# Searched orders for a gated recurrence and a causal convolution on one core: which engine gates the input, and in which order each engine works

## The chip, the cores and the metric

The kernel runs on one core of a Trainium2 chip. A core has TensorE (PE) for matmuls, VectorE (DVE), ScalarE (ACT) for activations, GpSimd (POOL), and SyncE (SP), which here issues the loads and stores. Each engine works through its own queue in order, and the engines wait for each other through semaphores. The metric is the device time of one execution in microseconds (us). The kernel before took 312.61 us, the median of 6 runs (311.6 to 314.11).

## The reference, cut to what matters

The input has 4 sequences of 6336 steps with 256 channels, 25344 rows in all. First comes a gated linear recurrence:

```python
log_a = c * sig_r * np.log(np.clip(a_base, 1e-06, 1.0 - 1e-06))[None, None, :]
a_t = np.exp(log_a)
norm = np.sqrt(np.maximum(1.0 - a_t * a_t, 1e-06))
x_gated = norm * sig_i * x
for t in range(S):
    h = a_t[:, t] * h + x_gated[:, t]
    y[:, t] = h
```

Its output goes through a causal convolution of five taps per channel, whose sigmoid gates a projection, and through an output projection:

```python
for k in range(K):
    gate_pre += conv_w[k][None, None, :] * xp[:, k:k + S, :]
gate = 1.0 / (1.0 + np.exp(-gate_pre))
val = x @ w_val
return (gate * val @ w_out).astype(np.float32)
```

## The kernel before, in words

Rows are cut into 51 tiles of 512 (three of them have 256), and tiles into 28 chunks of one or two tiles. Chunk 0 is tile 0, chunk 1 is tile 1, chunk 2 is tiles 2 and 3, and so on. Steps on channels-by-time data work by chunk and by half (`h` = 0 or 1, 128 channels each), numbered k = 2 x chunk + half. Square roots work by batches of two chunks, 14 in all.

A tile goes through these steps, named as in the code:

- `load` (L264, two DMAs for the two gates) and `loadx` (L271), issued by SP; `tanh` on ScalarE (L348) makes both gates.
- `u2` gates the input: (1 + tanh) times x. The string `U2` has one letter for each tile. With P, GpSimd does it in two instructions, L363 and L364. With D, VectorE does it in one fused instruction (L359) for each half of a tile.
- `srT` on TensorE (L373) transposes a gate, `exp` on ScalarE (L382) makes the decay a, `e` on GpSimd (L390) squares it, and `sq` on ScalarE (L394) takes the root for a batch. The root needs another activation table than `tanh` and `exp`, so there is a table load of 1.28 us before and after each `sq`.
- `nT` (L404) transposes the norm back, `xg` on VectorE (L411) multiplies it with the gated input, `xT` (L420) transposes the product, and `scan` on VectorE (L438) runs the recurrence.
- `conv` (L464, TensorE), `tg` (L472, ScalarE), `val` (L480, TensorE), `gv` (L490, VectorE), `out` (L502, TensorE); then the eviction `osb`, on VectorE (L513) or ScalarE (L515) by the letters of the string `OSB`, one for each half tile; and `store` (L520, SP).

The order of each engine's queue is written out as a string of letters in `ORDER`, one string for each engine; a letter stands for the next job of its kind on that engine. `make_plan` checks that the strings do not wait for each other. Its costs (`COST`) set only the order in which the instructions of different engines are emitted. Four PSUM banks serve `srT`, `nT`, `xT` and `out`, in the order of `BANK_ORDER`: a transpose into a bank waits until the earlier content has been read, that is for an `exp`, `xg`, `scan` or `osb`.

Buffers add waits. `tanh` of tile g writes the input gate's place of tile g - 5, so it waits for `u2` of that tile. `loadx` of tile g waits for `u2` of tile g - 4, and `load` for `tanh` of tile g - 4. `store` waits for its evictions, and what stands behind it on SP waits with it. The weights of the two projections are loaded by six DMAs that GpSimd issues (L527, L530), directly behind `e` 1 in its queue.

Of the kernel before, what the change touches and what calls it, by code (L numbers as in the profile page):

```python
# [29 lines left out]
BANKS = 4  # L30
PB = dict(srT=2, nT=2, xT=2, ops=2)

OSB = "DDDDDDDDDDDDDDDDDDDDDDDDDDDDDDDDDDDDDDDDDDDDDDDDDDDDDADDDDDDDDDDDDDDDDDDDDAAAAADDDDDAAAAAAAAAAADADA"

U2 = "DDDDPDPDDPPPPPPPPPPPDPPPPPPPPPPPPPPPPPPPPPPPPPPPPPP"

COST = dict(load=(0.05, 2.72), loadx=(0.02, 1.37), tanh=(0.11, 1.7), u2P=(0.2, 3.25), u2D=(0.2, 1.7), srT=(0.05,
            0.47), exp=(0.26, 0.86), e=(0.06, 1.83), sq=(0.2, 1.71), nT=(0.05, 0.53), xg=(0.02,
            0.58), xT=(0.04, 0.46), scan=(0.13, 2.14), conv=(0.15, 1.08), tg=(0.1, 0.83), val=(0.02,
            0.88), gv=(0.07, 1.07), out=(0.02, 0.43), osbD=(0.6, 0), osbA=(0.5, 0), store=(0.03,  # L40
# [3 lines left out]
LETTERS = dict(  # L44
    DMA=dict(l="load", x="loadx", s="store"), ACT=dict(t="tanh", e="exp", q="sq", g="tg", o="osb"),
    PE=dict(r="srT", n="nT", x="xT", c="conv", v="val", o="out"), POOL=dict(e="e", u="u2"),
    DVE=dict(u="u2", x="xg", s="scan", v="gv", o="osb"))
ORDER = dict(
    DMA=("lllxlllxlxlxxlxlxxlllxxlxlxsxxlsxlxllssxxlslxsxsllxxlsxssllslsxxxlsllssxslxlslsxxsllxslxslsxxsxslllx"
         "slxsxssllxlxxsxsslslxllsxsxsxllsxslxssxsxxsssssssssss"),  # L50
    ACT=("teeteetqtteteetetgqteegtteettgqgetegetetgqgteegttgetegtgeqgteetgetgqgetettgeegtgqeegttgtegetgtegqegt"
         "tgeetgtegqegttegetgoetgqegttegetgqgetegtgetgetgqeogetgootgoeoteegeqgeogeoqogogoogogooooggoo"),
    PE=("rrrrrrnxnrxrcxvxrcvrnnxnrxrnoocxxvcornrnvnocorxronvcxvooxcxronnvrocnovxncrvxroocxrocvooxvocrononcxrn"
        "voroxconvxocvornonnrcvonxrxvorcoxocovroxvxcrvnooncooxvrocxrvocnnoorcoovxcoorvnxvonocrxvrocoxvnrocono"
        "vxoxcrvonnocxrrxvoocnnrxcovroxovconvonnxrxcrnovcxroocvoxooovcrnnonxocxrvcrvoncovoxocovronxvrnncxnovo"
        "cxroovxrrcorovxoocovnonrcxrovonxcxnnvxocovocxxovcoxovooxcovcovoo"),
    POOL="eeeeeeeeueueeeuuueeeeuuuueeeueuuueeeeuueeeeuuueeuueeuueueueeueueueueeuueueeuuueeueeuuueueeeeuueeeuu",
    DVE=("uxsuxsussuvxuxusxsvxooussovxxvxoosxovsvoosoxxsovoxvxssoovsoovosovooxxusxvoosoxvsooxoxvxvxossovoosoov"
         "svsxooxvoosvosoxovoxoovsoovxsoxvosvoosovxoxovossxxovossoxxvsovosovxooxvxssxovsoovoosoovxxoxsovsvxoov"
         "oosovxsxxvsxvsvsoovoosoxxvsvxsxxvssvssvsvsovvo"))  # L60
BANK_ORDER = ("2123321110130102331302130221230122302301230123012121132131023123012102312123210310103201301301320131"
              "2023103130123102130231201213202310203123132010303132031321023031231202302001302313021231120312310321"
              "20131232130321320112030212312010312032010301231210212310312231")

WEIGHTS_AFTER = ("e", 1)
TABLE, SEM, DMA_LAT = 1.3, 0.15, 2.2
# [2 lines left out]
BF16 = mybir.dt.bfloat16  # L69
ACT = mybir.ActivationFunctionType  # L70
ALU = mybir.AluOpType
# [60 lines left out]
def make_jobs(sh):  # L132
# [9 lines left out]
    def job(op, eng, f, deps, cost=None, bank=0):  # L142
        fix, per = COST[cost or op]
        jobs[op].append((eng, fix + per * f, [d for d in deps if d[1] >= 0], bank))

    for g, (_, n) in enumerate(sh.tiles):
        f = n / WIN
        c = sh.chunk_of[g]
        job("load", "DMA", f, [("tanh", g - NIN)])
        job("loadx", "DMA", f, [("u2", g - NX)])  # L150
        job("tanh", "ACT", f, [("load", g), ("u2", g - NTI)]
            + ([("srT", 2 * sh.chunk_of[g - NTR] + 1)] if g >= NTR else []))
        job("u2", "DVE" if U2[g] == "D" else "POOL", f, [("tanh", g), ("loadx", g)] + ([("xT", 2 * sh.chunk_of[g - NU] + 1)] if g >= NU else []), "u2" + U2[g])
        job("nT", "PE", f, [("sq", unit_of[c]), ("xg", g - PB["nT"])], None, 1)
        job("xg", "DVE", f, [("nT", g), ("u2", g)])
        job("conv", "PE", f, [("scan", 2 * c + 1), ("tg", g - 1)])
        job("tg", "ACT", f, [("conv", g), ("gv", g - 2)])
        job("val", "PE", f, [("scan", 2 * c + 1), ("gv", g - 1), ("conv", g)])
        job("gv", "DVE", f, [("tg", g), ("val", g)] + ([("out", qlast[g - 2])] if g >= 2 else []))
        job("store", "DMA", f, [("osb", q) for q, (w, _) in enumerate(sh.pieces) if w == g])  # L160
    for c, (_, n, g0, g1) in enumerate(sh.chunks):
# [3 lines left out]
        for h in range(2):  # L165
            k = 2 * c + h
            job("srT", "PE", f, [("tanh", g1 - 1), ("exp", k - PB["srT"])], None, 1)
            aold = ("scan", 2 * sh.aold[c] + h if sh.aold[c] >= 0 else -1)
            job("exp", "ACT", f, [("srT", k), aold])
            job("e", "POOL", f, [("exp", k), ("sq", eu), ("nT", sh.chunks[ed][3] - 1 if ed >= 0 else -1)])  # L170
            job("xT", "PE", f, [("xg", g1 - 1), ("scan", k - PB["xT"])], None, 1)
            job("scan", "DVE", f, [("xT", k), ("val", ylast - 1), ("conv", ylast)])
    for q, (g, i) in enumerate(sh.pieces):
        job("out", "PE", 1, [("gv", g), ("osb", q - PB["ops"])], None, 1)
        job("osb", "DVE" if OSB[q] == "D" else "ACT", 1, [("out", q), ("store", g - NOSB)], "osb" + OSB[q])
    for u, n in enumerate(UNITS):
        size = sum(sh.chunks[c][1] for c in range(ends[u] - n, ends[u])) / CHUNK
        fix, per = COST["sq"]
        jobs["sq"].append(("ACT", fix * len(sh.runs[u]) + per * size, [("e", 2 * ends[u] - 1)], 0))
# [3 lines left out]
def make_plan(sh):  # L183
# [5 lines left out]
    for eng, letters in ORDER.items():  # L189
        todo = {op: [i for i, job in enumerate(jobs[op]) if job[0] == eng] for op in LETTERS[eng].values()}  # L190
        seq[eng] = [(op, todo[op].pop(0)) for op in (LETTERS[eng][x] for x in letters)]
        assert not any(todo.values())
    free_bank = iter(BANK_ORDER)
    for op, i in seq["PE"]:
# [5 lines left out]
    done, order, mode = {}, [], "E"  # L200
    free = dict(dict.fromkeys(seq, 0.0), DMA=START, ACT=ACT_START)
    at, left = dict.fromkeys(seq, 0), sum(len(ops) for ops in seq.values())
    while left:
        was = left
        for eng, ops in seq.items():
            while at[eng] < len(ops):
# [9 lines left out]
                free[eng] = t + dur  # L216
                done[op, i] = t + dur + (DMA_LAT if eng == "DMA" else 0.0)
                order.append((t, op, i, eng, dur))
# [351 lines left out]
```

## Time and profile before

| what | us |
|---|---|
| median of the runs | 312.61 |
| the profiled execution | 312.68 |
| its span, from the first to the last instruction | 310.8 |
| ScalarE busy | 289.1 |
| VectorE busy | 272.1 |
| TensorE matmul busy | 244.5 |
| GpSimd busy | 243.6 |
| DMA: share of 16 engines' time of the main queue | 88.2% |

Times in the profile count from the span's start. A group's row gives the line, the engine, the operation, what it writes and reads, the count, the busy time and mean nanoseconds, and then the idle time of the engine just before these instructions, with what ended it. In a timeline, each row has start, length, engine, line, operation, and in brackets the idle time before. In the 40 slices one digit stands for the busy tenths of 7.8 us.

### The profile page before, as it was taken

Reading aid. Unit: us, or ns where it says so; the run is one execution under the profiler, and the core shown is the slowest. Engines: PE = TensorE matmul, PEld = TensorE weight load, DVE = VectorE, ACT = ScalarE, POOL = GpSimd, SP = SyncE. Lnnn points to the kernel's source line nnn. Section 1 sums busy time; section 2 is a strip of 40 time slices with the busy share of each in tenths; the row PEclk is TensorE's granted clock in tenths of the full one; section 3 lists DMA queues with packets and bytes.
Section 4 is the critical chain, followed back from the end, with each engine's and each line's share of the span. In section 5 each row is a group of like instructions: output and inputs, shape, how many; then the busy total and the mean of one; then the engine's idle time right before and its main releaser. Section 6 shows DMA issues by size and latency. Waiting matters only on the chain.

```text
span 310.8 us, 6573 instructions
## 1 busy us (share of the span) xinstructions
PE 244.5 (79%) x2559; PEld 160.7 (52%) x2591; DVE 272.1 (88%) x279; ACT 289.1 (93%) x225; POOL 243.6 (78%) x154
## 2 busy tenths in 40 slices
PE   1127565789788858987899889888897998999994
PEld 1115243466555545654566555555564766656563
DVE  3008957989999999999999989999999899999973
ACT  6799699999999996999999999999999999999762
POOL 0907719999998999549999999899999989987300
PEclk9999897999999997999999999999999999999999
DMA  6999999999899999699999999997989999673145
GB/s 224 399 370 390 368 310 402 394 372 414 280 365 351 345 365 410 223 366 421 372 331 358 356 419 418 412 392 271 390 310 331 363 418 413 248 263 136 70 182 226
DMA packets 30797, 104.51 MB, mean 336 GB/s; under 512 B 4391, under 2 KB 4654, under 8 KB 30766
## 3 DMA queue, kind: packets, MB, share of 16 engines
q1 hardware_dynamic: 29376, 103.82, 88.2%
q0 software_dynamic: 1376, 0.26, 1.0%
q8 instruction: 20, 0.33, 0.4%
q14 instruction: 11, 0.09, 0.1%
q10 hardware_dynamic: 14, 0.01, 0.0%
HBM read 78.39 MB, written 25.95 MB: 336 GB/s over the span
## 4 chain that ended last, share of the span: by engine, by line
ACT 24%; DVE 21%; DMA 16%; issue 13%; PE 13%; POOL 10%; SPq 2%; DVEq 0%; ACTq 0%; POOLq 0%
DVE yring L438 9%; DMA ri<-in_i_gate_dram 8%; ACT tring L348 7%; ACT aring L382 5%; DMA out_dram<-osb 5%; POOL uring L364 5%; ACT ering L394 4%; DVE osb L513 4%; DVE gv L490 4%; PE gp L464 4%; PE bank L502 3%; ACT tg L472 3%; POOL ering L390 3%; POOL t L363 2%; DVE uring L411 2%
## 5 line engine op out<-in xcount | busy, mean ns | idle before, releaser
L390 POOL TENSOR_TENSOR ering<-aring 128x1024 f32<-128x1024 f32 (+2 forms) x56 | 95.2, 1714 | 40.9 <-ACT aring L382 40.1
L438 DVE TENSOR_TENSOR_SCAN yring<-aring,yring,bank 128x1024 bf16<-128x1024 f32 (+5 forms) x54 | 110.0, 2050 | 3.0 <-PE bank L420 2.9
L364 POOL TENSOR_TENSOR uring<-t,xt 128x1024 bf16<-128x1024 f32 (+1 forms) x43 | 100.1, 2328 | 3.6
L348 ACT ACTIVATE tring<-ri 128x2048 bf16<-128x2048 f32 (+1 forms) x51 | 94.2, 1868 | 3.7 <-issue 2.6
L464 PE MATMUL gp<-yring,diag 64*64 64x512 bf16 (+14 forms) x1196 | 67.5, 353 | 2.4 <-ACT tg L472 1.8
L382 ACT ACTIVATE aring<-bank,khf 128x1024 f32<-128x1024 bf16 (+2 forms) x56 | 61.1, 1111 | 3.7 <-PE bank L373 3.1
L502 PE MATMUL bank<-wo,gv 128*128 128x256 bf16 x396 | 58.6, 276 | 6.9 <-DVE yring L438 2.1
L490 DVE SCALAR_TENSOR_TENSOR gv<-tg,val 128x1024 bf16<-128x1024 bf16 (+1 forms) x54 | 60.4, 1122 | 2.7 <-PE val L480 2.0
L472 ACT ACTIVATE tg<-gp 128x1024 bf16<-128x1024 f32 (+1 forms) x51 | 51.3, 1007 | 5.2 <-PE gp L464 4.4
L373 PE MATMUL bank<-ident_b,tring 128*128 128x128 bf16 x396 | 34.5, 231 | 27.4 <-ACT tring L348 19.2
L513 DVE TENSOR_SCALAR osb<-bank 128x512 f32<-128x512 f32 x80 | 52.8, 679 | 3.2 <-PE bank L502 2.1
L480 PE MATMUL val<-yring,wv 128*128 128x512 bf16 (+1 forms) x172 | 47.7, 376 | 4.1 <-DVE gv L490 2.0
L502 PEld LDWEIGHTS <-gv 128*128 128x128 bf16 x396 | 36.7, 99 | 24.3 <-issue 11.5
L394 ACT ACTIVATE ering<-ering,b 128x4096 bf16<-128x4096 f32 (+4 forms) x16 | 46.8, 2934 | 0.2
L411 DVE TENSOR_TENSOR uring<-bank,uring 128x1024 bf16<-128x1024 bf16 (+1 forms) x51 | 33.2, 665 | 15.4 <-PE bank L404 15.2
L363 POOL TENSOR_SCALAR t<-tring 128x1024 f32<-128x1024 bf16 (+1 forms) x43 | 45.0, 1046 | 1.7
L373 PEld LDWEIGHTS <-tring 128*128 128x128 bf16 x396 | 28.0, 104 | 35.3 <-ACT tring L348 20.8
L464 PEld LDWEIGHTS <-diag 64*64 64x64 bf16 x1196 | 30.9, 109 | 27.7 <-issue 13.0
L404 PE MATMUL bank<-ident_f,ering 128*128 128x128 f32 x198 | 34.9, 304 | 12.5 <-ACT ering L394 5.6
L404 PEld LDWEIGHTS bank<-ident_f,ering 128*128 128x128 f32 x198 | 27.8, 207 | 20.3 <-ACT ering L394 7.7
L420 PE MATMUL bank<-ident_f,uring 128*128 128x128 f32 x198 | 33.6, 288 | 5.6 <-DVE uring L411 2.4
L420 PEld LDWEIGHTS bank<-ident_f,uring 128*128 128x128 f32 x198 | 22.8, 145 | 16.2 <-DVE uring L411 4.6
(32 smaller groups left out, 106.2 us busy)
## 6 DMA issues: line engine op xcount, KB each, us to landing
ri<-in_r_gate_dram SPq DMA_DIRECT2D x48, 512.0 KB, 7.7
ri<-in_i_gate_dram SPq DMA_DIRECT2D x48, 512.0 KB, 8.2
xt<-in_x_dram SPq DMA_DIRECT2D x48, 512.0 KB, 8.4
out_dram<-osb SPq DMA_DIRECT2D x48, 512.0 KB, 6.1
ri<-in_r_gate_dram SPq DMA_DIRECT2D x3, 256.0 KB, 6.2
ri<-in_i_gate_dram SPq DMA_DIRECT2D x3, 256.0 KB, 7.6
xt<-in_x_dram SPq DMA_DIRECT2D x3, 256.0 KB, 5.1
out_dram<-osb SPq DMA_DIRECT2D x3, 256.0 KB, 2.1
```

What stands on the lines that cost most here:

```text
L348: nc.scalar.activation(out=tring[:, r:i + 1:i - r, 0:nj, :], in_=ri[:, :, 0:nj, :], func=ACT.Tanh, scale=0.5)
L364: nc.gpsimd.tensor_tensor(out=u.rearrange("p w d e -> p w e d"), in0=t1.rearrange("p (w e) d -> p w e d", e=2), in1=xt.rearrange("p (w e) ...
L373: nc.tensor.transpose(out=srT[:, col:col + P], in_=tring[:, g % NTR, j, h * P:(h + 1) * P], identity=ident_b[:])
L382: nc.scalar.activation(out=aring[:, h, a0:a0 + nt].rearrange("c (w p j) -> c w p j", p=P, j=nj), in_=live.pop(("srT", k))[:, 0:nt].rearran ...
L390: nc.gpsimd.tensor_tensor(out=ering[:, H * e0 + h * nt:H * e0 + (h + 1) * nt], in0=a, in1=a, op=ALU.mult)
L404: nc.tensor.transpose(out=nT[:, w * D + h * P:w * D + (h + 1) * P], in_=ering[:, n0 + w:n0 + nw * P:nw], identity=ident_f[:])
L438: nc.vector.tensor_tensor_scan(out=yring[:, h, y0 + c0:y0 + c1], data0=aring[:, h, a0 + c0:a0 + c1], data1=xT[:, c0:c1], initial=0.0 if fr ...
L464: nc.tensor.matmul(out=gp[64 * h:64 * h + 64, m, c0:c1], lhsT=diag[rows, h, kk, rows], rhs=yring[rows, h, src:src + c1 - c0], start=(sh == 0),
L472: nc.scalar.activation(out=tg[:, :, 0:nt], in_=live.pop(("gp", g))[:, :, 0:nt], func=ACT.Tanh, scale=0.5)
L490: nc.vector.scalar_tensor_tensor(out=gv[:, 0:nj, hs, :].rearrange("c j h p -> c j (h p)"), in0=tg[:, hs, 0:nt].rearrange("c h (p j) -> c j ...
L502: nc.tensor.matmul(out=ops[:, e * D:(e + 1) * D], lhsT=gv[:, 2 * i + e, hk, :], rhs=wo[:, hk, :], start=(hk == 0), stop=(hk == H - 1))
L513: nc.vector.tensor_scalar(out=dst, in0=ops[:], scalar1=0.5, scalar2=None, op0=ALU.mult)
```

## The change

Three letters of `U2` go from D to P: tiles 5, 8 and 20. VectorE keeps the gated input of tiles 0, 1, 2, 3 and 7. Nine letters of `OSB` change; VectorE has 79 evictions instead of 80. The planner's cost of a gated input on VectorE goes from (0.2, 1.7) to (0.3, 3.3). With these, all five orders and the order of the banks are other strings. The work itself, the tiles, the buffers and the batches of roots stay.

```diff
-OSB = "DDDDDDDDDDDDDDDDDDDDDDDDDDDDDDDDDDDDDDDDDDDDDDDDDDDDDADDDDDDDDDDDDDDDDDDDDAAAAADDDDDAAAAAAAAAAADADA"
+OSB = "DDDDDDDDDDDDDDDDDDDDDDDDDDDDDDDDDDDDDDDDDDDDDADDDDDDDDDDDDDDDDDDDDDDDDDDAAAAADDAAAAAADDAAAAAADADA"
-U2 = "DDDDPDPDDPPPPPPPPPPPDPPPPPPPPPPPPPPPPPPPPPPPPPPPPPP"
+U2 = "DDDDPPPDPPPPPPPPPPPPPPPPPPPPPPPPPPPPPPPPPPPPPPPPPPP"
-... u2D=(0.2, 1.7) ...
+... u2D=(0.3, 3.3) ...
 ORDER = dict(
-    DMA=("lllxlllxlxlxxlxlxxlllxxlxlxsxxlsxlxllssxxlslxsxsllxxlsxssllslsxxxlsllssxslxlslsxxsllxslxslsxxsxslllx"
+    DMA=("lllxlxllxllxxlxxllxllxxlxxxllssllsxsxxsllxslxllsxlssxlxxslxslxlsxslsxxllsxxlxssxslslllxsslsxxsllxsls"
...
-    ACT=("teeteetqtteteetetgqteegtteettgqgetegetetgqgteegttgetegtgeqgteetgetgqgetettgeegtgqeegttgtegetgtegqegt"
+    ACT=("teteeetqtteteeetgtqgettetegetgqteetgteegttegqgettgetegetqgteegettgqgetetgtegetgqeegtgttgeegtgqegettg"
...
-    PE=("rrrrrrnxnrxrcxvxrcvrnnxnrxrnoocxxvcornrnvnocorxronvcxvooxcxronnvrocnovxncrvxroocxrocvooxvocrononcxrn"
+    PE=("rrrrnrnrxxrcrxxrvcvnnnxrxnrcroxocvrxoonovnrnxcnrocxrvocorovxocoxvrnnncxrvornxcrovoooxcovnrnxvorcrxvo"
...
-    POOL="eeeeeeeeueueeeuuueeeeuuuueeeueuuueeeeuueeeeuuueeuueeuueueueeueueueueeuueueeuuueeueeuuueueeeeuueeeuu",
+    POOL=("eeeeeeeeuuueeeeuuuueeeeuueueueeuueueeeuuuueeeeuueueueeuuueueueeeuueueeuuueeueueuuueeeuuueeeueuueeuu"
+          "ee"),
-    DVE=("uxsuxsussuvxuxusxsvxooussovxxvxoosxovsvoosoxxsovoxvxssoovsoovosovooxxusxvoosoxvsooxoxvxvxossovoosoov"
+    DVE=("uuxxssussvuxxxssxvuosovsoxooxxvsoxsvooovsoosxxvxsoxvsoovoosovxxsvosovsooxxovosxoovxsovosoovxxvoosoxs"
...
-BANK_ORDER = ("2123321110130102331302130221230122302301230123012121132131023123012102312123210310103201301301320131"
+BANK_ORDER = ("2023201312203123013103020312313010301320102020323213023213101323232312023132320131302312012302131001"
...
```

At the start, ScalarE's order "teeteetq" becomes "teteeetq": `exp` 1 stands behind `tanh` 1. VectorE's "uxsuxsuss" becomes "uuxxssuss". At the end, GpSimd's last two gated inputs stand ahead of the last two `e` instead of behind them, and ScalarE's queue has 13 jobs behind the last root instead of 17.

More of the change, by code (lines that the diff above doesn't have):

```diff
@@ L31 @@
 PB = dict(srT=2, nT=2, xT=2, ops=2)
-OSB = "DDDDDDDDDDDDDDDDDDDDDDDDDDDDDDDDDDDDDDDDDDDDDDDDDDDDDADDDDDDDDDDDDDDDDDDDDAAAAADDDDDAAAAAAAAAAADADA"
-U2 = "DDDDPDPDDPPPPPPPPPPPDPPPPPPPPPPPPPPPPPPPPPPPPPPPPPP"
-COST = dict(load=(0.05, 2.72), loadx=(0.02, 1.37), tanh=(0.11, 1.7), u2P=(0.2, 3.25), u2D=(0.2, 1.7), srT=(0.05,
+OSB = "DDDDDDDDDDDDDDDDDDDDDDDDDDDDDDDDDDDDDDDDDDDDDADDDDDDDDDDDDDDDDDDDDDDDDDDDAAAAADDDAAAAAADDAAAAAADADA"
+U2 = "DDDDPPPDPPPPPPPPPPPPPPPPPPPPPPPPPPPPPPPPPPPPPPPPPPP"
+COST = dict(load=(0.05, 2.72), loadx=(0.02, 1.37), tanh=(0.11, 1.7), u2P=(0.2, 3.25), u2D=(0.3, 3.3), srT=(0.05,
             0.47), exp=(0.26, 0.86), e=(0.06, 1.83), sq=(0.2, 1.71), nT=(0.05, 0.53), xg=(0.02,
@@ L48 @@
 ORDER = dict(
-    DMA=("lllxlllxlxlxxlxlxxlllxxlxlxsxxlsxlxllssxxlslxsxsllxxlsxssllslsxxxlsllssxslxlslsxxsllxslxslsxxsxslllx"
-         "slxsxssllxlxxsxsslslxllsxsxsxllsxslxssxsxxsssssssssss"),
-    ACT=("teeteetqtteteetetgqteegtteettgqgetegetetgqgteegttgetegtgeqgteetgetgqgetettgeegtgqeegttgtegetgtegqegt"
-         "tgeetgtegqegttegetgoetgqegttegetgqgetegtgetgetgqeogetgootgoeoteegeqgeogeoqogogoogogooooggoo"),
-    PE=("rrrrrrnxnrxrcxvxrcvrnnxnrxrnoocxxvcornrnvnocorxronvcxvooxcxronnvrocnovxncrvxroocxrocvooxvocrononcxrn"
-        "voroxconvxocvornonnrcvonxrxvorcoxocovroxvxcrvnooncooxvrocxrvocnnoorcoovxcoorvnxvonocrxvrocoxvnrocono"
-        "vxoxcrvonnocxrrxvoocnnrxcovroxovconvonnxrxcrnovcxroocvoxooovcrnnonxocxrvcrvoncovoxocovronxvrnncxnovo"
-        "cxroovxrrcorovxoocovnonrcxrovonxcxnnvxocovocxxovcoxovooxcovcovoo"),
@@ L57 @@
-    POOL="eeeeeeeeueueeeuuueeeeuuuueeeueuuueeeeuueeeeuuueeuueeuueueueeueueueueeuueueeuuueeueeuuueueeeeuueeeuu",
-    DVE=("uxsuxsussuvxuxusxsvxooussovxxvxoosxovsvoosoxxsovoxvxssoovsoovosovooxxusxvoosoxvsooxoxvxvxossovoosoov"
-         "svsxooxvoosvosoxovoxoovsoovxsoxvosvoosovxoxovossxxovossoxxvsovosovxooxvxssxovsoovoosoovxxoxsovsvxoov"
-         "oosovxsxxvsxvsvsoovoosoxxvsvxsxxvssvssvsvsovvo"))
-BANK_ORDER = ("2123321110130102331302130221230122302301230123012121132131023123012102312123210310103201301301320131"
-              "2023103130123102130231201213202310203123132010303132031321023031231202302001302313021231120312310321"
-              "20131232130321320112030212312010312032010301231210212310312231")
+    DMA=("lllxlxllxllxxlxxllxllxxlxxxllssllsxsxxsllxslxllsxlssxlxxslxslxlsxslsxxllsxxlxssxslslllxsslsxxsllxsls"
+         "xxlxssllxslxssxslxlxlslsxssxxllssxxslsxssxsxsssssssss"),
@@ new lines @@
+    ACT=("teteeetqtteteeetgtqgettetegetgqteetgteegttegqgettgetegetqgteegettgqgetetgtegetgqeegtgttgeegtgqegettg"
+         "tegetogetgqetgtegetgqegtetgtegetgeqgetgtgetgetgqooegetogeoteogetegeqoogoogoeogqgoogogoooggoo"),
+    PE=("rrrrnrnrxxrcrxxrvcvnnnxrxnrcroxocvrxoonovnrnxcnrocxrvocorovxocoxvrnnncxrvornxcrovoooxcovnrnxvorcrxvo"
+        "cxnnoovoocxrvnocorxnovrxocrvoocnnvooxcronxrvnoxcxvocroxrcvncoovronoovoxrcnvxnoocvnrxcorvocoxrvoncoox"
+        "ocxorvnnnvxrocrnvocxvxorcoxoovnronocxvrrocoxvconrnovooxrcxonvcnovxcorxcrovncoonvoorxvoconnxvrxoncnvr"
+        "xocroovrorcxrxvocoovnnonoxcovxorcoovxcxvnonocxovcxoxvoxocovcovoo"),
@@ new lines @@
+    POOL=("eeeeeeeeuuueeeeuuuueeeeuueueueeuueueeeuuuueeeeuueueueeuuueueueeeuueueeuuueeueeueuuueeeuuueeeueuueeuu"
+          "ee"),
+    DVE=("uuxxssussvuxxxssxvuosovsoxooxxvsoxsvooovsoosxxvxsoxvsoovoosovxxsvosovsooxxovosxoovxsovosoovxxvoosoxs"
+         "xovsosovsvxoovoxoovosxvxoosxvsoovsovxoosoovxxsxvosxvossoovosxovxoosvoosvoxxovososxvoxovssovoxooxvoos"
+         "vxxsvxsxvsovosovsxxxvsvsovosxvsxsvssvsvovo"))
+BANK_ORDER = ("2023201312203123013103020312313010301320102020323213023213101323232312023132320131302312012302131001"
+              "0131203212320031202312302320323011321031231012310232123102012310321132031320132032103021302232310120"
+              "13202312012023100213320321031330231023010230210320030320130132")
```

## The prediction

> **What bounds the kernel now.** I read the busy shares first, then the 40 slices, then the waits of ScalarE and GpSimd, then the timelines around ScalarE's two longest holes. The page:
>
> ```profile
> span 310.8 us, 6573 instructions
> PE 244.5 (79%) x2559; PEld 160.7 (52%) x2591; DVE 272.1 (88%) x279; ACT 289.1 (93%) x225; POOL 243.6 (78%) x154
> DVE  3008957989999999999999989999999899999973
> ACT  6799699999999996999999999999999999999762
> POOL 0907719999998999549999999899999989987300
> L382 ACT ACTIVATE aring<-bank,khf 128x1024 f32<-128x1024 bf16 (+2 forms) x56 | 61.1, 1111 | 3.7 <-PE bank L373 3.1
> L364 POOL TENSOR_TENSOR uring<-t,xt 128x1024 bf16<-128x1024 f32 (+1 forms) x43 | 100.1, 2328 | 3.6
> ```
>
> ScalarE is the pace: from 13 us to its last square root (289 us) its holes over 0.15 us sum to 6.3 us. VectorE has no more room (6.6 us between 53 and 299 us). GpSimd has some: it waits 40.1 us for `exp`, 25 of them between 24 and 286 us. So a gain has to come out of ScalarE's 6.3 us or out of the drain behind it. Two holes make most of it. The first, from the timeline (start, length, what, idle time before):
>
> ```profile
> 7.73 1.18 POOL L390 TENSOR_TENSOR ering<-aring 128x256 f32<-128x256 f32 x2 [6.42 <-ACT aring L382]
> 8.85 3.06 POOL L527 DMA_DIRECT2D wv<-in_moe_w_val_dram  x4
> 11.90 1.21 POOL L530 DMA_DIRECT2D wo<-in_moe_w_out_dram  x2
> 13.10 2.07 POOL L390 TENSOR_TENSOR ering<-aring 128x512 f32<-128x512 f32 x2
> ...
> 16.32 1.57 ACT L394 ACTIVATE ering<-ering,b 128x1536 bf16<-128x1536 f32 x1
> ...
> 29.12 4.51 DVE L359 SCALAR_TENSOR_TENSOR uring<-tring,xt 128x512 bf16<-128x512 bf16 x2
> ...
> 33.71 1.91 ACT L348 ACTIVATE tring<-ri 128x2048 bf16<-128x2048 f32 x1 [2.63 <-issue]
> ```
>
> The page calls the 2.63 us "issue". The code says more: `tanh` of tile 7 takes the gate buffer that `u2` of tile 2 reads, and that `u2` (L359) ends at 33.63, 0.08 us before. The second hole:
>
> ```profile
> 110.30 5.09 DVE L359 SCALAR_TENSOR_TENSOR uring<-tring,xt 128x512 bf16<-128x512 bf16 x2
> 115.31 2.33 DVE L438 TENSOR_TENSOR_SCAN yring<-aring,yring,bank 128x1024 bf16<-128x1024 f32 x1
> ...
> 117.70 0.64 PE L373 MATMUL bank<-ident_b,tring 128*128 128x128 bf16 x8 [3.51 <-DVE yring L438]
> ...
> 118.38 1.20 ACT L382 ACTIVATE aring<-bank,khf 128x1024 f32<-128x1024 bf16 x1 [2.12 <-PE bank L373]
> ...
> 122.07 1.02 ACT L472 ACTIVATE tg<-gp 128x1024 bf16<-128x1024 f32 x1 [0.69 <-PE gp L464]
> ```
>
> Here `u2` of tile 20 holds VectorE for 5.1 us, the scan behind it is late, TensorE waits 3.5 us for the bank that this scan reads, and ScalarE 2.12 and 0.69 us for TensorE. Both long `u2` run while GpSimd is busy. With GpSimd idle (tiles 5 and 7, 42 to 46 us) an L359 instruction takes 0.69 us; beside it, 1.55 (tile 8) to 2.78 us (tile 20).
>
> **The change, part by part**
>
> *Three `u2` to GpSimd (tiles 5, 8, 20).* VectorE loses six L359 instructions, in busy time 1.39 + 3.09 + 5.17 = 9.65 us. GpSimd gains three pairs of L363 and L364: 3 x 3.42 = 10.3 us. The first two fall mostly into its wait of 8.55 us before 45.5 us, the third into 3.20 + 1.00 + 3.71 us between 128 and 140 us; if that cover were gone, they would delay the `e` products and, through them, each square root, whose last `e` ended only 0.4 to 2.1 us before it was needed. Tile 20 gone from VectorE ends the second hole: -2.1 - 0.7 = -2.8 us. From both sides: 0 if the scan is late for another reason, -2.8 if not. I take -2.8, since on VectorE's new queue nothing longer than a scan stands ahead of that scan. (A freed VectorE alone shortens nothing where ScalarE paces.)
>
> *The first tiles' order.* VectorE now does `u2` of tiles 0 and 1, `xg` 0 and 1, both scans of chunk 0, and then `u2` of tile 2; on TensorE `nT` 0 stands ahead of `srT` 4 instead of behind `srT` 5. Before, `nT` 0 ran at 22.4 behind transposes that waited for `tanh` 3. Now it runs when the first root is done. `nT` 1 still waits for `tanh` 3, the new bank order makes `xT` 0 wait for `xg` 1, and `srT` 6 for the scan; so scans at about 25.7 to 27.1 and `u2` of tile 2 from 27 to 31.6 at its old 4.5 us. `tanh` 7 is reached later than that (below), so its hole of 2.63 us goes. What stands behind the longer waits: `val` 0 is now behind `srT` 8, which waits for `tanh` 7, and `gv` 0 with `u2` of tile 3 behind it on VectorE; `u2` 3 then ends near 42 us, and `tanh` 8 is due near 43.5. Hidden, with little over a microsecond to spare.
>
> *A delay that the same order brings.* `exp` 1 now stands behind `tanh` 1 on ScalarE. That costs ScalarE nothing: it fills the 0.70 us for which `exp` 2 waited. But on GpSimd, in the built program too, the six weight DMAs stand behind `e` 1 and ahead of `e` 2 and 3. `e` 1 moves from 8.3 to 11.6 us (`tanh` 1 ends at 11.07, `exp` 1 takes 0.5). Then 0.6 for `e` 1, 3.06 + 1.21 for the DMA issues, 2.07 for `e` 2 and 3: 18.5 us. The first root, at 16.32 before, waits for that: +2.2 us. The bounds: 0 if the root's table load hid all of it, +3.3 (the whole shift of `e` 1) if that load hid nothing; `e` 3 ended 1.1 us before the table load did, so 2.2. The weights land 3.3 us later too; `val` 0 is now after `tanh` 7, so nobody waits. Together the start gives +2.2 - 2.6 = -0.4 us.
>
> *Evictions.* VectorE 80 to 79, ScalarE 19 to 20: one L515 instruction of 0.60 us, 0.5 us from start to start: +0.5 us on ScalarE. The others only change place.
>
> *Loads and stores.* Bytes and counts stay (51 each). On SP's queue the first `x` tiles move up: `x` 1 passes loads 4 and 5, so load 4 lands some 1.3 us later (0.5 MB, by the steps of 1.27 us between landings); it had 3.2 us of lead. `x` 13 to 25 move back by up to 4.5 MB. At 1.27 us per 0.5 MB that is 11.4 us for tile 19, which had landed 9.9 us before use; but its `u2` on GpSimd is also later, behind more products. Cost 0; if that cover is gone, up to 1.6 us there. The load of tile 10 no longer stands behind `x` 7, which held SP from 34.0 to 38.2 us: no gain by itself, `tanh` 10 did not wait.
>
> *Cost entry, other orders, banks.* The cost entry only changes the order of emission, not any engine's queue. ScalarE keeps its 28 table switches for the roots. The remaining small waits on TensorE (0.42, 0.24, 0.17 us) I leave as they are: 0, between -0.8 and, at the size of the biggest hole of that kind, +2.1 us.
>
> *The drain.* From the start of scan 48 (284.82) to the end it took 26.0 us. Behind that scan VectorE now has two more evictions (2 x 0.59) and one `xg` less (0.60): +0.6 us. As three root-independent evictions and one `tg` move ahead of the last root on ScalarE, the last `xg` is later but not late: `scan` 50 is ahead of it. Between -1.5 (one tile's `conv`, `val`, `out` fewer behind the last `nT`) and +1.5 I take 0 for both together: the start of that drain moves with ScalarE.
>
> Sum: -2.8 - 0.4 + 0.5 = -2.7, and -0.5 for VectorE's 10 us of relief where a scan or `gv` was a little late for TensorE (it can be 0 to -0.8, above): -3.2 us. The profiled execution took 312.68 us (span 310.8, 1.9 around it), the median of the runs is 312.61, so 309.5 us.
>
> **A rule against this change.** The row: a pair on GpSimd took 3.42 us, on VectorE 1.39 beside an idle GpSimd and up to 5.17 beside a busy one. The Trainium skill (GPSIMD Engine Reference, 4.1 Engine selection) wants elementwise work on VectorE and calls GpSimd about twice as slow for two inputs. As an estimate from that page, the three pairs would cost VectorE only half of GpSimd's 10.3 us, 5.1; tile 20's would end 3.4 us sooner, the second hole would not be due to it, and the sum would be near 312.3. I go by the row.
>
> **The rivals**
> - *The holes come back elsewhere* (no change). For: VectorE and ScalarE are both full, and each microsecond saved makes ScalarE arrive earlier at waits that it just missed, such as `tanh` 8 or the roots (leads 0.4 to 2.1). Against: VectorE has 10 us less to do. The -3.2 shrinks to about -0.5: 312.2.
> - *GpSimd becomes the bound* (slower). Its holes were 25 us and take 10.3 us more. If one `x` tile is loaded only when its `u2` is already due, GpSimd stands for a landing (8.4 us, the page's median for x); the roots have at most 2.1 us of lead, so ScalarE stops for 6.3 us: 315.8. It decides from about 5.3 us of standing on (2.1 of lead, 3.2 of gain). For: `x` 13 to 25 are later in the queue. Against: GpSimd is itself later there.
> - *VectorE was the pace* (faster still). Its 9.65 us come out in full where it was full: 303.0. Against: ScalarE's queue has no such holes to give.
> - *The weight DMAs cost more than I think*, and the first hole stays (+2.2 and no -2.6): 312.1; counted with the first rival.
>
> **How the numbers follow.** Forecast 0.53, holes elsewhere 0.19, GpSimd 0.20, VectorE 0.08. About 0.5% (1.6 us) is what a measurement of this kernel can tell from no change, so faster means under 311.0. Of the forecast's 0.53, 0.50 is under that; with 0.08 and a quarter of the second case, faster is 0.62. Same takes the rest of the second and a little of GpSimd's: 0.18. Slower 0.20. The likeliest's own range is 307 to 311.5. For 8 in 10 it reaches up to the middle of GpSimd's case, 314.5, and down to between the forecast and 303, to 305.5.
>
> **What would show it.** Right: no L359 instruction after 60 us; no hole over 1 us on ScalarE at tile 7's `tanh` nor at the `exp` that stood at 118 us; the first root at about 18.5 us behind the weight DMAs; GpSimd's wait for `exp` down from 40 towards 25 to 30 us; VectorE's busy time near 262 us. Wrong: roots that wait for `e`, GpSimd waiting for `x` loads, or holes of a microsecond and more at other lines of ScalarE.

## The result and the profile after

The changed kernel takes 310.12 us (median of 36 runs, 309.09 to 312.5). Over the same time, the kernel before took 312.34 us (78 runs). The ratio is 0.9934, with a 95% interval from 0.9921 to 0.9947: faster by 0.7%, about 2.1 us. The forecast was 309.5 us. (All ratios here leave out executions more than 1.5% above the fastest of their kernel; the medians are of all executions.)

The profiled execution took 309.09 us, with a span of 307.3 us. It is the fastest of the 36, and the profiled one of before (312.68) was slightly over its median. So the traces show 3.6 us between the two kernels where the medians show 2.2. The page:

```profile
span 307.3 us, 6589 instructions
PE 241.7 (79%) x2558; PEld 159.2 (52%) x2591; DVE 262.3 (85%) x272; ACT 289.0 (94%) x226; POOL 253.1 (82%) x160
DVE  3035489859897989999999999999999999999993
ACT  5869999999999999999999999999999999998962
POOL 0643997999999999989899999999999989899100
L383 ACT ACTIVATE aring<-bank,khf 128x1024 f32<-128x1024 bf16 (+2 forms) x56 | 61.6, 1113 | 1.9 <-PE bank L374 1.3
L365 POOL TENSOR_TENSOR uring<-t,xt 128x1024 bf16<-128x1024 f32 (+1 forms) x46 | 107.2, 2330 | 3.8
```

ScalarE's work is the same, 289 us, in a span that is 3.5 us shorter. VectorE lost 9.8 us of work, GpSimd gained 9.5. (Lines of the changed kernel stand one further down: L365 is the L364 of before.) The timelines of the start and of the place of the second hole:

```profile
11.36 0.61 POOL L391 TENSOR_TENSOR ering<-aring 128x256 f32<-128x256 f32 x1 [2.98 <-ACT aring L383]
11.92 3.05 POOL L528 DMA_DIRECT2D wv<-in_moe_w_val_dram  x4
14.97 1.21 POOL L531 DMA_DIRECT2D wo<-in_moe_w_out_dram  x2
16.17 2.88 POOL L391 TENSOR_TENSOR ering<-aring 128x512 f32<-128x512 f32 x2
...
19.08 1.57 ACT L395 ACTIVATE ering<-ering,b 128x1536 bf16<-128x1536 f32 x1 [3.00 <-POOL ering L391]
...
27.87 2.04 DVE L360 SCALAR_TENSOR_TENSOR uring<-tring,xt 128x512 bf16<-128x512 bf16 x2
...
34.01 1.92 ACT L349 ACTIVATE tring<-ri 128x2048 bf16<-128x2048 f32 x1
...
37.24 3.71 ACT L395 ACTIVATE ering<-ering,b 128x4096 bf16<-128x4096 f32 x1
...
113.53 1.22 ACT L383 ACTIVATE aring<-bank,khf 128x1024 f32<-128x1024 bf16 x1
114.61 3.73 ACT L349 ACTIVATE tring<-ri 128x2048 bf16<-128x2048 f32 x2
118.22 1.04 ACT L473 ACTIVATE tg<-gp 128x1024 bf16<-128x1024 f32 x1
```

Both holes of before are gone: `tanh` of tile 7 (34.01) and the `exp` and `tg` between 113 and 119 have no idle time before them. A new one stands at the first root: 3.00 us, behind the weight DMAs between `e` 1 and `e` 2, which GpSimd now issues at 11.92 us instead of 8.85. The second root starts at 37.24 instead of 37.42, so the start of the kernel has gained almost nothing. The second hole's 2.8 us is most of the gain in the traces. The rest is smaller: a wait of 0.42 us at 191 us is gone, those at 282 to 286 us are 1.1 us longer in sum (the largest is 0.92 us before an `exp`), and those behind the last root 1.5 us shorter.

### The profile page after: what moved, and what is told of

The parts are those of the page before. It is cut to its first block, busy times and chain, and to the rows that moved or that the text cites. A ratio compares the mean times of both kernels' runs of the same rounds, so it can differ in the third digit from the quotient of the medians.

```text
span 307.3 us, 6589 instructions
## 1 busy us (share of the span) xinstructions
PE 241.7 (79%) x2558; PEld 159.2 (52%) x2591; DVE 262.3 (85%) x272; ACT 289.0 (94%) x226; POOL 253.1 (82%) x160
## 4 chain that ended last, share of the span: by engine, by line
ACT 43%; PE 14%; DVE 14%; DMA 13%; issue 11%; POOL 3%; SPq 1%; ACTq 0%; DVEq 0%
ACT tring L349 15%; DMA ri<-in_i_gate_dram 11%; ACT aring L383 7%; ACT ering L395 7%; ACT tg L473 7%; DVE yring L439 6%; PE gp L465 4%; DVE gv L491 3%; PE val L481 3%; PE bank L503 3%; ACT L395 2%; DMA ri<-in_r_gate_dram 2%; ACT L383 2%; DVE uring L412 2%; PE bank L405 2%
## 5 line engine op out<-in xcount | busy, mean ns | idle before, releaser
L391 POOL TENSOR_TENSOR ering<-aring 128x1024 f32<-128x1024 f32 (+2 forms) x56 | 95.2, 1713 | 26.3 <-ACT aring L383 25.8
L365 POOL TENSOR_TENSOR uring<-t,xt 128x1024 bf16<-128x1024 f32 (+1 forms) x46 | 107.2, 2330 | 3.8
L364 POOL TENSOR_SCALAR t<-tring 128x1024 f32<-128x1024 bf16 (+1 forms) x46 | 47.6, 1035 | 1.9
L405 PE MATMUL bank<-ident_f,ering 128*128 128x128 f32 x198 | 34.0, 302 | 17.2 <-ACT ering L395 14.1
L374 PEld LDWEIGHTS <-tring 128*128 128x128 bf16 x396 | 27.3, 102 | 29.6 <-ACT tring L349 17.9
L421 PE MATMUL bank<-ident_f,uring 128*128 128x128 f32 x198 | 32.1, 281 | 2.2 <-ACT aring L383 1.2
L481 PEld LDWEIGHTS <-wv 128*128 128x128 bf16 x204 | 19.8, 101 | 15.8 <-issue 3.9
```

The source lines that it names most:

```text
L365: nc.gpsimd.tensor_tensor(out=u.rearrange("p w d e -> p w e d"), in0=t1.rearrange("p (w e) d -> p w e d", e=2), in1=xt.rearrange("p (w e) ...
L391: nc.gpsimd.tensor_tensor(out=ering[:, H * e0 + h * nt:H * e0 + (h + 1) * nt], in0=a, in1=a, op=ALU.mult)
L405: nc.tensor.transpose(out=nT[:, w * D + h * P:w * D + (h + 1) * P], in_=ering[:, n0 + w:n0 + nw * P:nw], identity=ident_f[:])
L481: nc.tensor.matmul(out=val[:, m, 0:nt], lhsT=wv[:, hk, m * P:(m + 1) * P], rhs=yring[:, hk, y0:y0 + nt], start=(hk == 0), stop=(hk == H - 1))
```

## The experiments

In all runs the comparison is with the kernel before, run on the same chip in the same rounds.

**The weight DMAs behind the fourth `e`** (on the changed kernel)

```diff
-WEIGHTS_AFTER = ("e", 1)
+WEIGHTS_AFTER = ("e", 3)
```

> The changed kernel with the six weight DMAs of GpSimd behind the fourth e instead of the second. Theory: in the changed kernel the first root waits 3.0 us for e 3, which stands behind 4.3 us of DMA issues; GpSimd then stands idle for 7.8 us before e 4. Moved into that idle time the issues cost nothing: the root starts at about 16.1 us (behind its table load) instead of 19.1, and the rest follows, about 2.5 to 3 us less than the changed kernel, 307.3 us by the median. Rival: the start is set by something behind it as well (the gated input of tile 2 for tanh of tile 7, or the loads), a hole opens at that tanh, and at most 1 us is left of it, 309.2 us.

Measured: 307.38 us, ratio 0.9828 (0.9793 to 0.9864). On ScalarE:

```profile
15.99 1.57 ACT L395 ACTIVATE ering<-ering,b 128x1536 bf16<-128x1536 f32 x1
...
34.95 3.71 ACT L395 ACTIVATE ering<-ering,b 128x4096 bf16<-128x4096 f32 x1
...
65.87 1.21 ACT L383 ACTIVATE aring<-bank,khf 128x1024 f32<-128x1024 bf16 x1 [1.17 <-PE bank L374]
```

The first root no longer waits. By the medians the theory's number is met: the new hole cost the changed kernel some 2.7 us. The rival fell, as no hole opened at `tanh` of tile 7 and the second root is 2.3 us earlier than in the changed kernel. The trace says less than the medians: behind the second root ScalarE waits 0.24, 0.45 and 1.17 us for TensorE (the last was 0.17 us in the changed kernel), and at the fourth root only 0.3 us are left (81.61 against 81.94). This profiled execution (308.83) is the slowest of its six, and that of the changed kernel the fastest of its 36.

**`exp` 1 ahead of `tanh` 1 again** (on the changed kernel, weights where they were)

```diff
-    ACT=("teteeetq...
+    ACT=("teeteetq...
```

> The changed kernel with one swap in ScalarE's order: exp 1 ahead of tanh 1 again, as before the change. Theory: e 1 is then done near 8.9 us, the weight DMAs behind it are issued while GpSimd would stand idle, the first root starts near 16.1 us instead of 19.1, and the time is that of the kernel with the weights behind the fourth e, 307.4 us. Rival: that kernel gained because the weight loads came later and left the first input loads more bandwidth; then this one, where they come 3 us earlier than in the changed kernel, stays near 310.

Measured: 307.24 us, ratio 0.9835 (0.9808 to 0.9863). The start of this kernel, from its timelines:

```profile
7.44 1.18 POOL L391 TENSOR_TENSOR ering<-aring 128x256 f32<-128x256 f32 x2 [6.14 <-ACT aring L383]
8.57 3.06 POOL L528 DMA_DIRECT2D wv<-in_moe_w_val_dram  x4
...
16.07 1.58 ACT L395 ACTIVATE ering<-ering,b 128x1536 bf16<-128x1536 f32 x1
...
28.43 1.20 ACT L383 ACTIVATE aring<-bank,khf 128x1024 f32<-128x1024 bf16 x1 [0.68 <-PE bank L374]
...
35.03 3.71 ACT L395 ACTIVATE ering<-ering,b 128x4096 bf16<-128x4096 f32 x1
```

The weights are issued at 8.57 us, earlier than in any kernel above, and the time is that of the run with the latest issue (14.61 us). So what counts is not when the weights load but what stands behind their issue on GpSimd. Of the 3.0 us at the first root, 2.2 are left at the second (35.03 against 37.24), since `exp` 7 now waits 0.68 us for TensorE. The hole of 1.17 us at 65 us is here too (0.17 in the changed kernel). This profiled execution (307.91) is among the slower of its six.

**The weight DMAs at the very start** (on the changed kernel)

```diff
-WEIGHTS_AFTER = ("e", 1)
+WEIGHTS_AFTER = ("tanh", 0)
```

> The changed kernel with the six weight DMAs issued behind the planned start of the first tanh, that is ahead of GpSimd's first e, where GpSimd waits 6.5 us for the first exp. Theory (only the issue time in front of e 2 and e 3 counts): no root waits, 307.4 us. Rival (the weight transfers themselves, small packets, hold back the first gate loads, for which tanh of tile 1 waited 1.2 us): tanh of tile 1 later by 0.7 to 3 us, 308 to 310 us.

Measured: 308.18 us, ratio 0.9862 (0.9833 to 0.9891). The issues lie in GpSimd's idle time (1.45 to 5.7 us) and no root waits, but `tanh` of tile 1 waits 2.03 us for its gates instead of 1.23 and starts at 9.51 instead of 8.92:

```profile
9.51 1.91 ACT L349 ACTIVATE tring<-ri 128x2048 bf16<-128x2048 f32 x1 [2.03 <-DMA ri<-in_i_gate_dram]
```

The first theory holds: the issue time is hidden. That the transfers delay the first gate, as the rival has it, is not shown. In the run with a sixth place (below), which issues the weights behind `e` 1, this `tanh` starts still later (9.73, after 1.91 us of waiting), and the interval overlaps those of the two runs above.

**Tile 20 alone to GpSimd** (on the kernel before)

```diff
-U2 = "DDDDPDPDDPPPPPPPPPPPDPPP...
+U2 = "DDDDPDPDDPPPPPPPPPPPPPPP...
-    POOL="eeeeeeeeueueeeuuueeeeuuuueeeueuuueeeeuueeeeuuu...
+    POOL="eeeeeeeeueueeeuuueeeeuuuueeeueuuueeeeuuueeeeuuu...
-    DVE=("...ovosovooxxusxvoosox...
+    DVE=("...ovosovooxxsxvoosox...
```

> The kernel before with one letter changed: the gated input of tile 20 goes to GpSimd, behind e 23, and out of VectorE's queue; nothing else moves. Theory: the hole of 2.12 and 0.69 us on ScalarE near 118 to 122 us goes, 2.8 us less than before: 309.6 us. GpSimd's wait of 3.2 us near 128 us takes the pair in. Rival (the hole comes back elsewhere, as VectorE and ScalarE are both full): within 0.5 us of before, 312.2 us. Second rival (VectorE's 5 us come out in full): 307.2 us.

Measured: 308.92 us, ratio 0.9876 (0.9839 to 0.9912). The edit is one letter moved from one queue to another, and it gives 3.8 us. On ScalarE:

```profile
114.95 1.03 ACT L472 ACTIVATE tg<-gp 128x1024 bf16<-128x1024 f32 x1
115.86 1.22 ACT L382 ACTIVATE aring<-bank,khf 128x1024 f32<-128x1024 bf16 x1
116.94 1.93 ACT L348 ACTIVATE tring<-ri 128x2048 bf16<-128x2048 f32 x1
118.74 1.04 ACT L472 ACTIVATE tg<-gp 128x1024 bf16<-128x1024 f32 x1
```

The second hole is gone, and nothing takes its place. The first hole stays (2.63 us before `tanh` 7, as in before). The gain is 1 us over the two waits. In the traces 0.3 us of it is there from the start, and the wait of 0.42 us at 191 us in the kernel before is gone too; the rest is open. This one letter beats the whole change: the intervals of the two ratios do not meet.

**All three tiles to GpSimd, all other orders as before**

```diff
-U2 = "DDDDPDPDDPPPPPPPPPPPDPPP...
+U2 = "DDDDPPPDPPPPPPPPPPPPPPPP...
-    POOL="eeeeeeeeueueeeuuueeeeuuuueeeueuuueeeeuueeeeuuu...
+    POOL="eeeeeeeeuueueeeuuuueeeeuuuueeeueuuueeeeuuueeeeuuu...
-    DVE=("uxsuxsussuvxuxusxsvxooussovxx...
+    DVE=("uxsuxsussuvxxusxsvxoossovxx...
```

> The kernel before with all three letters changed (tiles 5, 8 and 20 to GpSimd, each put into GpSimd's queue beside its neighbours) and every other order as before. Theory (ScalarE paces, GpSimd has room except between 50 and 128 us): tile 5 falls into the idle 8.5 us and costs nothing; tile 8 puts 3.4 us ahead of e 12 to 15, whose lead over the third to fifth roots was 0.4 to 0.8 us plus a table load of 1.3, so up to 2 us of the gain of tile 20 alone (308.9 us) is lost: 310 to 311 us, with a root that waits for e. Rival (GpSimd takes it all): 308.9 us or less. Second rival (VectorE's relief counts too): 307 us.

Measured: 309.62 us, ratio 0.9912 (0.9886 to 0.9937). It is a little behind tile 20 alone, and the intervals overlap. No root waits for `e`, so the loss expected there is not what happened. What the trace shows instead is that GpSimd's longer work now lies beside VectorE's tiles 3 and 7: 3.08 instead of 2.23 us and 3.58 instead of 1.30 us. `exp` 11 then waits 0.65 us for TensorE:

```profile
45.81 3.58 DVE L359 SCALAR_TENSOR_TENSOR uring<-tring,xt 128x512 bf16<-128x512 bf16 x2
...
52.75 1.20 ACT L382 ACTIVATE aring<-bank,khf 128x1024 f32<-128x1024 bf16 x1 [0.65 <-PE bank L373]
```


**A sixth place for the input gate** (on the kernel before)

```diff
-NU = 10
+NU = 9
-NTI = 5
+NTI = 6
```

> The kernel before with six places for the input gate instead of five (and nine instead of ten for the gated input, whose waits had 12 us to spare), so that tanh of tile 7 waits for the gated input of tile 1, not of tile 2. All orders stay. Theory: the page's 2.63 us of issue before tanh of tile 7 were a wait for VectorE's gated input of tile 2 (4.5 us beside GpSimd); tanh of tile 7 starts at about 31.2 us, the second root at about 34.8 instead of 37.4, and the time falls by 2 to 2.6 us, to 310.0 us. Rival: the hole is one of the load or of issuing and stays: 312.3 us.

Measured: 315.42 us by the median, ratio 1.0061 (1.0024 to 1.0098), slower. The hole went as expected. The second root starts at 35.27 instead of 37.42, which shows that the page's "issue" was the wait for VectorE's `u2` of tile 2. Then the gain was given back, and more. From this run's timelines:

```profile
35.27 3.71 ACT L394 ACTIVATE ering<-ering,b 128x4096 bf16<-128x4096 f32 x1
...
43.37 1.89 POOL L390 TENSOR_TENSOR ering<-aring 128x1024 f32<-128x1024 f32 x1 [5.80 <-ACT aring L382]
43.95 3.33 DVE L359 SCALAR_TENSOR_TENSOR uring<-tring,xt 128x512 bf16<-128x512 bf16 x2
...
55.21 4.19 DVE L359 SCALAR_TENSOR_TENSOR uring<-tring,xt 128x512 bf16<-128x512 bf16 x2
...
69.36 1.02 ACT L472 ACTIVATE tg<-gp 128x1024 bf16<-128x1024 f32 x1 [1.57 <-PE gp L464]
```

ScalarE is 2.1 us earlier, so GpSimd gets its next `e` at 43.37 instead of 45.53, and it now works while VectorE gates tile 7. That pair takes 3.33 us instead of 1.30, and tile 8's 4.19 instead of 3.01. VectorE loses 3.2 us, and ScalarE then waits 0.65 us at `exp` 11 and 1.57 us at `tg` 4, both for TensorE. The first follows from VectorE's loss, as TensorE waits 1.60 us for its scan just before (49.59 us). For `tg` 4 this is only argued, from the order of events. By the fourth root the gain is gone (78.5 against 78.0 us), and the second hole is 0.6 us longer (2.41 and 1.00 us). This kernel's runs lie in two groups, from 312.4 to 313.2 and from 315.4 us up; the profiled one took 313.22, and what the longer ones add is open.

**Both edits on the kernel before**: tile 20 to GpSimd and the sixth place.

> Both edits on the kernel before: tile 20's gated input on GpSimd and the sixth place for the input gate. If the two holes are separate and ScalarE alone sets the pace, their gains add: 5.4 us less than before, 306.9 us, which would be under the changed kernel's 310.1. If another engine or the loads are nearly as full, the second gain is smaller than the first: 309 us.

Measured: 312.6 us by the median, with runs from 308.1 to 314.8; ratio 0.9954 (0.9917 to 0.9992). The gains do not add: with the second edit, more than half of what tile 20 alone gives is lost by the ratio, and nearly all of it by the medians. Why the runs spread so is open.

**GpSimd emptied** (on the kernel before; `e` and GpSimd's gated inputs cut to two columns each)

```diff
-            nc.gpsimd.tensor_tensor(out=u.rearrange(...), in0=t1.rearrange(...), in1=xt.rearrange(...), op=ALU.mult)
+            nc.gpsimd.tensor_scalar(out=u[:, 0, 0:1, :], in0=xt[:, 0:1, 0:2], scalar1=1.0, scalar2=None, op0=ALU.mult)
...
-            nc.gpsimd.tensor_tensor(out=ering[:, H * e0 + h * nt:H * e0 + (h + 1) * nt], in0=a, in1=a, op=ALU.mult)
+            nc.gpsimd.tensor_tensor(out=ering[:, H * e0 + h * nt:H * e0 + h * nt + 2], in0=a[:, 0:2], in1=a[:, 0:2], op=ALU.mult)
...
+        nc.gpsimd.memset(uring[:], 0.0)
+        nc.gpsimd.memset(ering[:], 0.0)
```

> The kernel before with GpSimd's work cut to two columns an instruction: its e squares and its gated inputs are left out but for these, and their buffers are filled once at the start; all queues and waits but the one of tanh for GpSimd's gated input stay, VectorE's work is whole. Only the lengths of VectorE's fused gated input (L359 before) are read from it. Theory: an instruction of it takes 0.69 us alone and up to 2.78 us because GpSimd works at the same time, so all of tiles 1, 2, 3, 5, 7, 8 and 20 take about 1.4 us a tile here. Rival: it is slow because of the loads or of ScalarE and TensorE, or because of where its buffers lie: then tiles 2 and 20 stay at 4 to 5 us.

The instructions of VectorE's gated input by their line, the kernel before first (15 instructions: shortest, median, longest in ns), then the emptied one:

```profile
L359 DVE SCALAR_TENSOR_TENSOR uring<-tring,xt x15: 689/1544/2778, 12.4 to 113.0; 128x512 bf16<-128x512 bf16 x15
```

```profile
L361 DVE SCALAR_TENSOR_TENSOR uring<-tring,xt x15: 675/697/702, 21.7 to 122.2; 128x512 bf16<-128x512 bf16 x15
```

With GpSimd idle every one of the 15 takes 0.68 to 0.70 us, tiles 2 and 20 too, while the DMA engines, ScalarE and TensorE went on working (115 to 120 us, just ahead of tile 20: DMA share 1.02, ScalarE 4.97 and TensorE 4.43 of 5 us). GpSimd is the cause. (The run took 320.92 us; the two fills hold up its start, and its first gated input begins at 21.7 us instead of 12.4.)

## Why the prediction was right, point by point

- *The bound.* Right. ScalarE's 289 us stayed and its holes shrank, from 6.3 to 4.7 us between 13 us and the last root and from 6.5 to 4.9 behind it; what VectorE lost (9.8 us) did not come out.
- *Tile 20, -2.8 us.* Right in place and kind, and confirmed by the edit alone, which gave 3.8 us. From the fifth to the sixth root ScalarE gained 3.0 us on before in the trace.
- *The first tiles, -2.6 us.* The hole of `tanh` 7 closed. One figure was off: `u2` of tile 2 was put at its old 4.5 us and took 2.04, as it met one running `e` of GpSimd (26.84 to 28.74 us) instead of two. That had no effect, since `tanh` 7 came later than either.
- *The weight DMAs, +2.2 us.* Right in mechanism, undersized: `e` 1 started at 11.36 (forecast 11.6), but `e` 2 and 3 took 2.88 us instead of 2.07, beside VectorE's gated input of tile 1 (15.98 to 18.1 us). The root came at 19.08 instead of 18.5, 2.8 us later than before. Undoing it is worth 2.7 to 2.9 us by the medians and 3.1 to 3.3 by the ratios, more than the change gained. Start in all: -0.2 us by the second root, forecast -0.4.
- *Loads.* Cost 0, right: `x` of tile 19 landed 4.9 us before its use, because that use moved from 109 to 117 us.
- *Evictions and relief, +0.5 and -0.5 us.* Neither shows as such. ScalarE's busy time did not grow, and its small waits behind the second hole became longer, not shorter: 0.4 us went and 1.1 us came.
- *The drain.* Forecast 0 (with +0.6 us for VectorE's evictions in it), measured -0.5: from scan 48 (281.81) to the end it took 25.5 us, before the change 26.0.
- *The rule against the change.* The measured time is on the side of the rows. The rule of the Trainium skill (GPSIMD Engine Reference, 4.1 Engine selection) holds here for VectorE alone: 1.39 us a pair against 3.42 on GpSimd. Beside a busy GpSimd the pair took up to 5.17 us.
- *The rivals.* No root waited for `e` except the first, so GpSimd did not become the bound; its wait for `exp` fell from 40.1 to 25.8 us, the low end of what was forecast. "The holes come back elsewhere" was wrong for the change, where only the 1.1 us at 282 to 286 us came back, but the sixth buffer shows that it is a real case: there, an earlier ScalarE brought GpSimd's work beside VectorE's.
- *Size.* The sum of -3.2 us is near the traces (-3.6) and was 1 us too large for the change as measured (-2.1). Its nearness to the traces is partly luck: they compare the fastest execution of the changed kernel with a middling one of the kernel before, and the 0.6 us that the weights cost beyond the forecast were made up by the drain. What the other executions add is open.

The version that beats both kernels is the changed one with the weight DMAs out of the way of `e` 2 and 3: 307.2 to 307.4 us by either of two edits.

## What to carry to other kernels

Before a search over orders, look for what the planner does not know: here six DMA issues on GpSimd, 4.3 us in a queue, which the new orders moved so late that the first root waited for what stood behind them. An operation's time that depends on what another engine does at that moment is no constant in a plan; when a wait is removed, ask which pairs of engines now meet. And undo a large change in parts: one letter of this one was worth more than all of it.

## What the runs showed of the hardware

VectorE's gated input has both inputs in SBUF, and beside GpSimd it took 0.69 to 2.78 us. Its `xg`, `gv` and `scan`, which read one input from PSUM, did not change: 681, 1211 and 2336 ns in the kernel before, 683, 1213 and 2339 ns with GpSimd emptied. That agrees with the Trainium skill (GPSIMD Engine Reference, 8. Key points), which says that GpSimd shares its SBUF interfaces with VectorE, with contention for VectorE instructions that have two SBUF inputs or use a two-port mode. How much it costs is read from these runs, and there it is a wait rather than a slower rate. Tile 20 in the kernel before, its two instructions and GpSimd's beside them:

```profile
110.15 2.38 POOL L364 TENSOR_TENSOR uring<-t,xt 128x1024 bf16<-128x1024 f32 x1
110.30 2.78 DVE L359 SCALAR_TENSOR_TENSOR uring<-tring,xt 128x512 bf16<-128x512 bf16 x1
112.47 2.37 POOL L390 TENSOR_TENSOR ering<-aring 128x1024 f32<-128x1024 f32 x1
113.00 2.40 DVE L359 SCALAR_TENSOR_TENSOR uring<-tring,xt 128x512 bf16<-128x512 bf16 x1
```

Each of VectorE's two ends some 0.56 us behind the end of the GpSimd instruction that was running when it began. The same holds for all eight slowed ones of the kernel before (0.55 to 0.56 us); the other seven, which began while GpSimd ran no such instruction, took 0.69 to 0.70. So what a gated input costs depends on how much of GpSimd's instruction is left when it begins. It works both ways: the two `e` of chunk 1 took 2.07 us alone and 2.88 beside a gated input. The strongest case came unasked. In the emptied kernel, two fills by GpSimd lie beside VectorE's first small copies, whose inputs are in SBUF alone:

```profile
1.24 8.63 POOL L334 MEMSET uring<- 128x10240 bf16 x1
9.80 8.63 POOL L335 MEMSET ering<- 128x10240 f32 x1
```

```profile
1.32 17.19 DVE L287 CAST ident_b<-ident_f 128x128 bf16<-128x128 f32 x1 [1.32 <-POOL ident_f masks.py:199]
3.08 15.44 DVE L301 TENSOR_SCALAR ksig<-kexp 128x2 f32<-128x2 f32 x1
```

The cast took 0.23 us in the kernel before. Here it ended at 18.5 us, just behind the second fill (18.4): like the gated inputs it was held until GpSimd's instruction had ended, here two of them. This was seen once.
